# Channel product of a fused attention, gating and rotation block: from eight row tiles to seven block products per pair

## The chip, the cores and the metric

The kernel runs on one core of a Trainium2 chip, as one program in one launch. The metric is the device time of that core in microseconds. The kernel before took 833.74 us, the median of three runs (832.26 to 833.87).

## What is computed

The batch has B = 8 items of S = 576 tokens; the model width is 512 and everything is float32. Three stages follow each other. The reference, cut to what matters:

```python
p_packed = sm_attn(p, k, v)                 # attention of 32 packed queries per head
x = sm_attn(q, p_packed, p_packed)          # attention back to 576 tokens, 8 heads of 64

h = np.maximum(x @ w_in, 0.0)               # gating stage, d_ff = 1024
u, v = h[..., :512], h[..., 512:]
v_n = (v - mean(v)) / np.sqrt(var(v) + 1e-06)            # layer norm over the width
v_s = einsum('ts,bsd->btd', w_spatial, v_n) + b_spatial[None, :, None]
x = (u * v_s) @ w_out

theta = x @ w_theta                         # rotation stage
zr, zi = x * np.cos(theta), x * np.sin(theta)
u = x + einsum('ts,bsd->btd', w_tok_r, zr) + einsum('ts,bsd->btd', w_tok_i, zi)
return u + np.maximum(u @ w_ch, 0.0)        # the channel product is u @ w_ch
```

## The kernel before

Float32 precision is kept on TensorE by splitting: every operand is stored as a high part `h` (rounded to the matmul's format) and a low part `l = x - h`, and a product is three matmuls, h·h, h·l and l·h. Each split costs one ScalarE instruction for the high part (`hi`, L519) and one subtraction on VectorE or GpSimd for the low part (`lo`; all VectorE and GpSimd instructions bear the recorder's line, L507).

**First phase.** A loop over the eight batch items computes both attentions (`first`, `second`), the gating input product (`m_part`, `u_part`, `v_part`), the layer norm (inside `v_part`, whose inner function `rsq` finds 1/sqrt(var + eps) on five columns) and the spatial product (`g_part`), which goes out to a DRAM tensor `Gd`. In between, the weights of the later stages are converted from the float64 in which they arrive (`cvt_tasks`), split, combined and, as far as they are needed in blocks, stored to DRAM (`wr_part` to `Wd`; `wc_part` keeps `w_ch` split in SBUF as `WC`). The first 34 us are filled up with 70 matmuls on the identity that feed nothing (L1242).

**Second phase.** It works on four pairs of batch items (p = 0 to 3). A pair has nine row tiles of 128 rows: four of the first item (j = 0 to 3), one that holds the last 64 rows of both (j = 4), four of the second (j = 5 to 8). `X` makes x and theta of two tiles (`x_pair`: a 2x2 block product with seven instead of eight block products; the first six tiles go through `x_tile`), and `rotate` takes theta to cosine and sine: VectorE rounds the angle to whole turns by adding and subtracting a large constant (a TENSOR_SCALAR) and subtracts (a TENSOR_TENSOR), ScalarE takes Abs, Sin and Sin, two products follow. `mix(p, n)` with n = 1, 2, 6, 7, 4, 5, 3 is the token mixing of a pair in seven block products (`product`, weights loaded from `Wd` as `wg` tiles, operands split into `op` tiles). Its results are gathered in the `xs` tiles, which then hold u.

**The channel product.** `C(p, j)` takes one finished row tile of u. `turn` (L1598) transposes it by four TensorE instructions into a PSUM bank and splits it from there into a `uT` tile (high part on ScalarE, low part on VectorE). `chan` (L1608) multiplies: four blocks of the width times three terms are 12 matmuls, 128x128 by 512 columns, with `uT` as the stationary operand and `WC` as the moving one. VectorE then does max(., 0) + u in one instruction from PSUM and the tile is stored. There are 36 tiles, so 432 such matmuls.

**The order of the work.** Nothing is scheduled at run time. Every task is added to a plan (`P.add`, L432) and gets its place from a table of numbers, `PLACES` (L33), and, where two engines can do it, its engine from the table `ENGINES` (L351). `run` (L453) emits the tasks in order of their places, so the tables fix each engine's queue. `run` also ties a GpSimd task behind the VectorE task that stands ahead of it (the code gives as reason "order of the shared port"). Tiles come from pools (8 PSUM banks; `op` 5, `wg` 3, `xs` 13, `fa` 20, `tt` 2, `uT` 2); a task that needs a new tile waits until one is free.

```python
            for k in range(4):
                for x, y in ((0, 0), (1, 0), (0, 1)):
                    mm(ps.t, uT.t[:, x * 512 + k * 128:x * 512 + (k + 1) * 128], WC[y][:, k, :], m == 0, m == 11)
```

Of the kernel before, what the change touches and what calls it, by code (L numbers as in the profile page):

```python
# [21 lines left out]
NPAIR = B // 2  # L22
# [4 lines left out]
RSQRT_SEED = float(0x5F3759DF)  # L27
# [11 lines left out]
    "chan DVE": [  # L39
        1785, 1615, 1883, 1800, 1816, 1929, 1881, 2045, 1941, 2085, 2061, 2176, 2183, 2279, 2261, 2304, 2332, 2375,  # L40
        2419, 2483, 2526, 2593, 2671, 2748, 2631, 2752, 2780, 2869, 2831, 2833, 2876, 2875, 2880, 2891, 2867, 2887,
        2888],
    "chan mms": [
        1573, 1604, 1841, 1776, 1810, 1917, 1873, 1947, 1931, 2064, 2032, 2163, 2171, 2267, 2251, 2292, 2319, 2355,
        2410, 2434, 2510, 2577, 2660, 2708, 2625, 2745, 2721, 2754, 2779, 2828, 2850, 2866, 2873, 2886, 2855, 2878],
    "chan st": [
        1807, 1690, 1889, 1823, 1820, 1973, 2015, 2069, 1946, 2091, 2063, 2190, 2187, 2283, 2265, 2307, 2346, 2408,
        2421, 2521, 2531, 2596, 2712, 2749, 2633, 2782, 2784, 2883, 2834, 2838, 2879, 2885, 2884, 2892, 2881, 2890,
        2889],
    "cvt_tasks a": [  # L50
        65, 74, 42, 50, 164, 160, 174, 178, 241, 273, 349, 333, 339, 485, 407, 616, 470, 796, 814, 573, 882, 925,
        651, 1051, 1021, 673, 1144, 1292, 746],
# [58 lines left out]
    "load_tile DVE": [
# [10 lines left out]
    "m_part ACT": [  # L122
        120, 115, 157, 148, 216, 214, 234, 231, 323, 309, 305, 328, 478, 465, 463, 475, 640, 627, 629, 623, 783, 788,
# [389 lines left out]
def moe_kernel(ctx: ExitStack, tc, qT, kT, v, pT, w_in, wsT, bs, w_out,  # L513
# [1244 lines left out]
    for p in range(NPAIR):  # L1758
# [80 lines left out]
```

## Time and profile before

| | |
|---|---|
| median of three runs | 833.74 us (832.26 to 833.87) |
| profiled execution | 833.59 us, span from first to last instruction 831.6 us |
| granted TensorE clock | 0.999 of full speed (2.4 GHz) over the span |
| TensorE busy | 823.5 us, 99% of the span |
| VectorE busy | 631.3 us, 76% |
| ScalarE busy | 463.1 us, 56% |
| GpSimd busy | 218.9 us, 26% |
| DMA | 119 MB, 143 GB/s on average |

The span is cut by the profile into instructions of each engine; PE is TensorE, PEld its weight loads, DVE VectorE, ACT ScalarE, POOL GpSimd, SP the engine that issues the DMAs. A matmul's duration is longer than the distance to the next one, as they are pipelined, so what a matmul costs is read from a long row of them and not from its own duration. Identity matmuls and the like in full float32 count as two instructions in the profile.

### The profile page before, as it was taken

How to read it: one execution, taken by the hardware profiler on the slowest of the kernel's cores; microseconds unless marked ns; L12 is line 12 of the kernel's file. 1: busy time of each engine (PE TensorE's matmuls, PEld its weight loads, DVE VectorE, ACT ScalarE, POOL GpSimd, SP SyncE). 2: the span in 40 equal slices, each digit the busy share in tenths (PEclk: the TensorE clock that was granted, in tenths of full speed). 3: DMA queues.
4: the chain of work that ended last, by engine and by line, in shares of the span. 5: the costliest groups of instructions: out<-in, count | busy, mean ns of one | idle time of the engine just before them, and what ended most of it. 6: DMA issues, size and time to landing. Idle time of an engine off the chain costs nothing.

```text
span 831.6 us, 14720 instructions
## 1 busy us (share of the span) xinstructions
PE 823.5 (99%) x5490; PEld 684.9 (82%) x5490; DVE 631.3 (76%) x1260; ACT 463.1 (56%) x981; POOL 218.9 (26%) x176
## 2 busy tenths in 40 slices
PE   9999999999999999999999999999999999999998
PEld 7778888878787999887888888888888888888886
DVE  4998889988898895687886788854787756877534
ACT  4897767875585863774546355455553436434310
POOL 0342414224311311003122231233324134133310
PEclk9999999999999999999999999999999999999999
DMA  9986366577655158542061233333224233123412
GB/s 316 340 290 210 113 213 205 175 242 233 183 161 154 44 168 259 181 139 81 9 215 52 89 114 87 104 114 101 86 68 136 92 102 128 39 88 100 151 55 88
DMA packets 86859, 119.03 MB, mean 143 GB/s; under 512 B 10882, under 2 KB 57730, under 8 KB 86788
## 3 DMA queue, kind: packets, MB, share of 16 engines
q1 hardware_dynamic: 86788, 118.09, 44.9%
q8 instruction: 43, 0.70, 0.3%
q14 instruction: 28, 0.23, 0.1%
HBM read 88.38 MB, written 29.69 MB: 142 GB/s over the span
## 4 chain that ended last, share of the span: by engine, by line
PE 94%; DMA 2%; DVE 1%; ACT 1%; issue 1%; SPq 0%; POOL 0%; POOLq 0%; DVEq 0%
PE bank L525 91%; PE bank L1603 2%; DMA vr<-vL 1%; DMA WX<-Td 1%; PE bank L719 1%; DVE WX L507 1%; PE bank L746 0%; DMA Wd<-raw 0%; PE bank L1049 0%; POOL op L507 0%; DVE M L507 0%; DVE at L507 0%; PE bank L720 0%; DVE gs L507 0%; SPq L1199 0%
## 5 line engine op out<-in xcount | busy, mean ns | idle before, releaser
L525 PE MATMUL bank<-op,wg 128*128 128x512 f32 x672 | 174.7, 392 | 0.5 <-POOL op L507 0.5
L525 PE MATMUL bank<-WX,gp 128*128 128x512 f32 x630 | 155.4, 391 | 0.0
L525 PEld LDWEIGHTS bank<-op,wg 128*128 128x128 f32 x672 | 125.0, 188 | 26.2 <-POOL op L507 1.0
L525 PEld LDWEIGHTS bank<-WX,gp 128*128 128x128 f32 x630 | 117.6, 188 | 24.3
L507 DVE TENSOR_TENSOR xs<-bank,xs 128x256 f32<-128x256 f32 (+2 forms) x125 | 72.9, 591 | 71.6 <-PE bank L525 59.6
L525 PE MATMUL bank<-WS,VN 128*128 128x288 f32 x768 | 115.7, 298 | 0.0
L525 PEld LDWEIGHTS bank<-WS,VN 128*128 128x128 f32 x768 | 105.7, 188 | 8.6 <-issue 3.4
L525 PE MATMUL bank<-WC,uT 128*128 128x512 f32 x432 | 104.2, 391 | 0.0
L525 PEld LDWEIGHTS bank<-WC,uT 128*128 128x128 f32 x432 | 80.6, 188 | 16.6
L507 POOL TENSOR_TENSOR op<-fa,op 128x512 fp32r<-128x512 f32 x40 | 52.0, 1307 | 155.0 <-DVE op L507 70.6
L1451 ACT ACTIVATE xs<-bank 128x256 f32<-128x256 f32 x60 | 22.8, 380 | 107.6 <-PE bank L525 107.4
L519 ACT ACTIVATE op<-fa 128x512 fp32r<-128x512 f32 x96 | 58.6, 628 | 42.8 <-PE bank L525 26.5
L507 POOL TENSOR_TENSOR fa<-xs,fa 128x512 f32<-128x512 f32 x29 | 38.2, 1323 | 89.8 <-DVE fa L507 24.5
L525 PE MATMUL bank<-at,M 128*128 128x288 f32 x384 | 56.6, 299 | 0.0
L525 PE MATMUL bank<-M,at 128*128 128x512 f32 x224 | 55.5, 395 | 0.0
L525 PEld LDWEIGHTS bank<-at,M 128*128 128x128 f32 x384 | 52.1, 188 | 1.9 <-ACT ur L934 0.5
L507 DVE TENSOR_TENSOR op<-fa,op 128x512 fp32r<-128x512 f32 x56 | 42.4, 769 | 9.8 <-ACT op L519 9.4
L525 PEld LDWEIGHTS bank<-M,at 128*128 128x128 f32 x224 | 40.7, 188 | 8.8 <-issue 0.9
L519 ACT ACTIVATE uT<-bank 128x512 fp32r<-128x512 f32 x36 | 21.3, 596 | 46.8 <-PE bank L1603 28.8
L507 DVE TENSOR_TENSOR fa<-fa,fa 128x512 f32<-128x512 f32 x56 | 40.4, 722 | 4.2 <-POOL fa L507 2.7
L525 PE MATMUL bank<-op,WR 128*128 128x512 f32 x128 | 39.5, 390 | 0.0
L519 ACT ACTIVATE gp<-g 128x768 fp32r<-128x768 f32 (+1 forms) x30 | 28.2, 951 | 19.5 <-PE bank L525 18.9
(178 smaller groups left out, 1452.3 us busy)
## 6 DMA issues: line engine op xcount, KB each, us to landing
wg<-Wd SPq DMA_DIRECT2D x56, 512.0 KB, 4.1
kt<-kT SPq DMA_DIRECT2D x16, 576.0 KB, 7.0
q<-qT SPq DMA_DIRECT2D x16, 576.0 KB, 7.5
vr<-vL SPq DMA_DIRECT2D x16, 512.0 KB, 6.6
out<-xs SPq DMA_DIRECT2D x32, 256.0 KB, 2.7
g<-Gd SPq DMA_DIRECT2D x60, 128.0 KB, 3.1
Wd<-raw SPq DMA_DIRECT2D x56, 128.0 KB, 2.0
Gd<-gs SPq DMA_DIRECT2D x16, 288.0 KB, 2.3
```

The source lines that it names most:

```text
L507: self.made.append(f(*a, **k))
L519: A.activation(out=out, in_=in_, func=AF.Copy)
L525: PE.matmul(out, lhsT, rhs, start=start, stop=stop, skip_group_check=more)
L719: PE.transpose(p1.t[:, k * 128:(k + 1) * 128], a1.t[:, k * 128:(k + 1) * 128], ident)
L1451: A.activation(out=to[a].t[:, c], in_=bank.t[:, a * 256:(a + 1) * 256], func=AF.Copy)
L1603: PE.transpose(pt.t[:, d * 128:(d + 1) * 128], xs.t[:, d * 128:(d + 1) * 128], ident)
```

## The change

**Channel product of three pairs.** For p = 0, 1, 2 the eight row tiles j = 0 to 3 and 5 to 8 no longer go through `C`. A new function, `chan_pair`, transposes u of both items (32 TensorE transposes, as `turn` did), copies the result from PSUM to `xs` tiles, and treats it as a 2x2 block matrix (halves of the width by the two items). With w_ch as the other 2x2 block matrix, seven block products of 12 matmuls replace eight tiles of 12 matmuls. Four of the seven need sums of blocks of u (`sub7`), and four need sums of blocks of w_ch. The latter are made once in the first phase by `wc_pair` (which replaces `wc_part`), stored to a DRAM tensor `Cd`, and loaded as `wg` tiles. Sums of products are formed partly by accumulation in PSUM, partly by a ScalarE copy (`save`) and a VectorE addition (`gather`). The output of these rows is stored transposed and put right on the host by a copy; j = 4 and the whole last pair go the old way.

**The angle's rounding.** In `rotate`, ScalarE adds the large constant (`near`, Identity with a bias tile), and VectorE does the rest in one SCALAR_TENSOR_TENSOR; the sign is turned in the sine's scale.

**The layer norm's root.** ScalarE takes Ln and Exp (`root`), VectorE does one correction step instead of a seed and three steps; the table set with both functions is asked for at the start.

**The list anew.** `PLACES` and `ENGINES` are new for the whole kernel. The pools `fa` and `tt` are merged into `xs` (35 tiles).

```diff
+    def chan_pair(p, key):
+        u = {}
+        for o in range(2):
+            four = [xs[p, 5 * o + i] for i in range(4)]
+            for k in range(4):
...
+                def trs4(four=four, k=k, pt=pt):
+                    for i in range(4):
+                        PE.transpose(pt.t[:, i * 128:(i + 1) * 128], four[i].t[:, k * 128:(k + 1) * 128], ident)
+                P.add("PE", 0.37, trs4, key + k, r=four, new=[pt])
+                P.add("ACT", 0.62, lambda t=t, pt=pt: A.activation(out=t.t, in_=pt.t, func=AF.Copy), key + k + 1, r=[pt], new=[t])
+                u[o, k] = t
+        b11, b21, b12, b22 = ([u[o, 2 * n + kk] for kk in range(2)] for o in range(2) for n in range(2))
...
+        def prod7(k0, n0, load, x, ps, start, key):
...
+                P.add("SP", 0.6, lambda: SP.dma_start(out=wg.t.bitcast(F32), in_=Cd[load]), key - 6, r=[R_cd], new=[wg], size=0.524e6)
...
+            ops = [split(x[kk], P.res("op"), key - 4 + 0.7 * kk) for kk in range(2)]
+            for m in range(2):
+                for kk in range(2):
+                    def f7(m=m, kk=kk):
+                        o = ops[kk][0]
+                        three(ps[m].t, lambda y: lhs(kk, m, y), lambda y: o.t[:, y], start and not kk, kk == 1, not start)
...
+        def save(ps, key):
+            t = []
+            for m in range(2):
+                c = P.res("xs")
+                P.add("ACT", 0.62, lambda c=c, m=m: A.activation(out=c.t, in_=ps[m].t, func=AF.Copy), key, r=[ps[m]], new=[c])
...
+        def gather(c, ps, key):
+            for m in range(2):
+                P.add("DVE", 0.69, lambda m=m: V.tensor_tensor(out=c[m].t, in0=ps[m].t, in1=c[m].t, op=ALU.add), key,
+                      r=[ps[m], c[m]], w=[c[m]])
...
+        Aq, Yq, Cq = two(), two(), two()
+        prod7(0, 0, None, b11, Aq, True, key)
+        prod7(2, 0, None, b21, Yq, True, key + 2.7)
+        c = save(Yq, key + 6)
+        gather(c, Aq, key + 6.5)
+        done7(c, 0, 0, key + 7)
+        t = sub7(b12, b11, key - 2)
+        prod7(0, 0, 0, t, Cq, True, key + 5.4)
+        sub7(b22, t, key + 1, t)
+        prod7(0, 0, 1, t, Aq, False, key + 8.1)
+        t3 = sub7(b22, b12, key + 5)
+        e = save(Aq, key + 11)
+        prod7(0, 0, 2, t3, Aq, False, key + 10.8)
+        sub7(b21, t, key + 4, t)
+        c = save(Cq, key + 8)
+        gather(c, Aq, key + 14)
+        done7(c, 1, 1, key + 15)
+        prod7(2, 256, None, t, Aq, False, key + 13.5)
+        done7(None, 0, 1, key + 17, Aq)
+        prod7(0, 0, 3, b22, Cq, False, key + 16.2)
+        gather(e, Cq, key + 19)
+        done7(e, 1, 0, key + 20)
...
         mix(p, 3)
-        todo += [(p, 5), (p, 6), (p, 4)]
+        if p + 1 < NPAIR:
+            P.group = 10 * p + 9
+            chan_pair(p, clock + 2)
+            clock += 22
+            todo += [(p, 4)]
+        else:
+            todo += [(p, 5), (p, 6), (p, 4)]
...
+        def near():
+            A.activation(out=ab.t, in_=f.t, func=AF.Identity, bias=magic)
+        P.add("ACT", 0.62, near, key - 0.1, r=[f], new=[ab])
 
         def frac():
-            V.tensor_scalar(out=ab.t, in0=f.t, scalar1=MAGIC, scalar2=MAGIC, op0=ALU.add, op1=ALU.subtract)
-            V.tensor_tensor(out=f.t, in0=f.t, in1=ab.t, op=ALU.subtract)
-        P.add("DVE", 1.15, frac, key, r=[f], w=[f], new=[ab], port=True)
+            V.scalar_tensor_tensor(out=f.t, in0=ab.t, scalar=MAGIC, in1=f.t, op0=ALU.subtract, op1=ALU.subtract)
+        P.add("DVE", 0.7, frac, key, r=[ab, f], w=[f], port=True)
...
+        def root():
+            A.activation(out=t(), in_=cols(0, 10).rearrange("p (j c) -> p j c", c=2)[:, :, 1], func=AF.Ln, bias=lneps)
+            A.activation(out=y(), in_=t(), func=AF.Exp, scale=-0.5)
+        P.add("ACT", 0.5, root, key + 8.4, r=[st], w=[st])
```

**Where the order shows it.** TensorE, pair 0. Before, a tile of the channel product is four transposes and, ten instructions on, a row of 12 matmuls with `uT` as stationary operand (`xs` is the tile of u, `WC` the weight, `gp` and `WX` belong to `x_pair`, `z` and `WRR` to the mixing):

```order
L1603 MATMUL bank_171<-ident,xs_4089 128x128 x4
...
L525 MATMUL bank_166<-z_4235,WRR 128x512 x3
L525 MATMUL bank_173<-WC_72,uT_4239 128x512 x2
L525 MATMUL bank_173<-WC_73,uT_4239 128x512
L525 MATMUL bank_173<-WC_72,uT_4239 128x512 x2
L525 MATMUL bank_173<-WC_73,uT_4239 128x512
...
```

Of the change, the same place: groups of three matmuls on an `op` tile (split transposed u), with `WC` or a `wg` tile loaded from `Cd`, mixed with matmuls of `x_pair` and one old-style transposition of tile j = 4:

```order
L555 MATMUL bank_175<-op_4079,WC_75 128x512
L555 MATMUL bank_175<-op_4079,WC_76 128x512
L555 MATMUL bank_175<-op_4079,WC_75 128x512
L1675 MATMUL bank_173<-ident,xs_4095 128x128 x4
L555 MATMUL bank_172<-WX_3637,gp_3639 128x512
...
L555 MATMUL bank_176<-op_3902,wg_4258 128x512 x3
L555 MATMUL bank_176<-op_4078,wg_4258 128x512 x3
L555 MATMUL bank_169<-op_3902,wg_4258 128x512 x3
L555 MATMUL bank_169<-op_4078,wg_4258 128x512 x3
L555 MATMUL bank_171<-op_3903,wg_4260 128x512 x3
```

The transposes are as many as before (32 for the eight tiles of a pair); the matmuls with 512 columns behind them are 84 where 96 stood.

VectorE, the same stretch of the change: what stands between the transposed blocks and those matmuls. `xs<-xs,xs` are the sums of blocks, `op<-xs,op` low parts of a split, `xs<-bank` reads of PSUM, `z` belongs to the mixing of the next pair:

```order
L537 TENSOR_TENSOR xs_4264<-xs_4094,xs_4091 128x512
L537 TENSOR_TENSOR z_4257<-xs_4084,z_4257 64x512
L537 TENSOR_TENSOR xs_4083<-xs_4089,xs_4087 128x512
L537 TENSOR_TENSOR op_3902<-xs_4264,op_3902 128x512
L537 TENSOR_TENSOR xs_4264<-xs_4271,xs_4264 128x512
L537 TENSOR_TENSOR op_4078<-xs_4083,op_4078 128x512
L537 TENSOR_TENSOR xs_4268<-xs_4097,xs_4268 128x512
L537 TENSOR_TENSOR xs_4081<-xs_4271,xs_4094 128x512
L537 TENSOR_TENSOR op_3903<-xs_4264,op_3903 128x512
L537 TENSOR_TENSOR xs_4086<-bank_175,xs_4086 128x512
L537 TENSOR_TENSOR xs_4090<-bank_171,xs_4090 128x512
```

Before, VectorE had one low part and one max-and-add per tile here, both from PSUM; now sums and low parts from SBUF stand close together.

SP, the first loads of the program. Before, the value tiles `vr` of the first item stand ahead of most of the weight `w_in`:

```order
L688 DMA kt_113<-kT 128x2x576
L693 DMA vr_114<-vL 128x4x256
L694 DMA vr_114<-vL 64x256
L999 DMA wth<-w_in 128x1024 x2
L999 DMA woT<-w_in 128x1024
```

Of the change:

```order
L721 DMA kt_116<-kT 128x2x576
L1034 DMA woT<-w_in 128x1024
L1034 DMA wth<-w_in 128x1024 x2
L726 DMA vr_117<-vL 128x4x256
L727 DMA vr_117<-vL 64x256
```

Three loads of `w_in` moved ahead of the first `vr`.

## Rows read from the trace of the kernel before

**Rows 1.** The page: span, and busy time, share and instructions of each engine

```profile
span 831.6 us, 14720 instructions
...
PE 823.5 (99%) x5490; PEld 684.9 (82%) x5490; DVE 631.3 (76%) x1260; ACT 463.1 (56%) x981; POOL 218.9 (26%) x176
```

**Rows 2.** The page: chain that ended last, share of the span by engine

```profile
PE 94%; DMA 2%; DVE 1%; ACT 1%; issue 1%; SPq 0%; POOL 0%; POOLq 0%; DVEq 0%
```

**Rows 3.** Windows: length, PE, PEld, DVE, ACT, POOL busy (count), clock, DMA

```profile
0.00:40.00 40.00, 38.13 (x430) 29.56 (x431) 28.41 (x66) 24.33 (x61) 7.97 (x13) 1.00 0.99 332
...
80.00:340.00 260.00, 258.73 (x2375) 220.70 (x2374) 223.15 (x535) 176.44 (x393) 68.42 (x54) 1.00 0.56 178
...
600.00:700.00 100.00, 100.00 (x454) 82.82 (x453) 71.24 (x123) 49.28 (x97) 28.50 (x23) 1.00 0.32 96
```

**Rows 4.** Waits of PE: the view without four small waits, together 1.5 us

```profile
PE bank L525 <- POOL ident masks.py:199: 1.4, 1, 1.4
PE bank L525 <- ACT vf L876: 0.8, 1, 0.8
PE bank L525 <- POOL op L507: 0.5, 1, 0.5
```

**Rows 5.** Timeline of PE in the second phase: start, length, instruction, count

```profile
399.11 2.88 PE L525 MATMUL bank<-WC,uT 128*128 128x512 f32 x12
...
404.55 4.24 PE L525 MATMUL bank<-op,wg 128*128 128x512 f32 x18
```

**Rows 6.** Groups by line: count, busy us, mean ns; the channel product

```profile
L525 PE MATMUL bank<-WC,uT 128*128 128x512 f32 x432 | 104.2, 391 | 0.0
```

**Rows 7.** Groups by line: the instructions of 512 columns beside TensorE

```profile
L519 ACT ACTIVATE op<-fa 128x512 fp32r<-128x512 f32 x96 | 58.6, 628 | 42.8 <-PE bank L525 26.5 <-POOL fa L507 8.0 <-DVE fa L507 7.7
L507 POOL TENSOR_TENSOR op<-fa,op 128x512 fp32r<-128x512 f32 x40 | 52.0, 1307 | 155.0 <-DVE op L507 70.6 <-ACT op L519 25.8 <-DVE fa L507 24.6
L507 DVE TENSOR_TENSOR op<-fa,op 128x512 fp32r<-128x512 f32 x56 | 42.4, 769 | 9.8 <-ACT op L519 9.4
L507 DVE TENSOR_TENSOR fa<-fa,fa 128x512 f32<-128x512 f32 x56 | 40.4, 722 | 4.2 <-POOL fa L507 2.7
...
L507 DVE TENSOR_TENSOR uT<-bank,uT 128x512 fp32r<-128x512 f32 x36 | 24.6, 686 | 18.4 <-ACT uT L519 18.3
L507 DVE SCALAR_TENSOR_TENSOR xs<-bank,xs 128x512 f32<-128x512 f32 (+1 forms) x37 | 24.6, 671 | 13.7 <-PE bank L525 13.6
...
L1496 ACT ACTIVATE fa<-fa 128x512 f32<-128x512 f32 x36 | 22.5, 626 | 23.0 <-DVE fa L507 22.9
...
L507 DVE TENSOR_SCALAR fa<-fa 128x512 f32<-128x512 f32 x36 | 16.3, 453 | 8.8 <-ACT fa L1451 4.7 <-issue 1.9 <-ACT fa L1367 1.8
```

**Rows 8.** Groups by line: small instructions and table loads

```profile
L507 DVE SCALAR_TENSOR_TENSOR ln<-ln 128x5 f32<-128x5 f32 x56 | 9.2, 165 | 1.9
...
L1497 ACT ACT_TABLE_LOAD x1 | 1.3, 1283 | 0.0
...
L1238 ACT ACTIVATE one<-halfpi 128x1 f32<-128x1 f32 x1 | 0.2, 203 | 0.0
```

**Rows 9.** Windows: the second phase, and its 28 us with most VectorE work

```profile
736.00:764.00 28.00, 28.00 (x135) 23.25 (x134) 24.78 (x39) 14.27 (x27) 9.34 (x7) 1.00 0.32 101
...
360.00:832.00 472.00, 467.27 (x2130) 386.50 (x2128) 329.55 (x547) 213.22 (x411) 126.64 (x97) 1.00 0.32 99
```

**Rows 10.** Timeline: the end of the program

```profile
819.37 8.45 PE L525 MATMUL bank<-WC,uT 128*128 128x512 f32 x36
...
827.86 0.69 DVE L507 SCALAR_TENSOR_TENSOR xs<-bank,xs 128x512 f32<-128x512 f32 x1 [1.96 <-PE bank L525]
```

**Rows 11.** Timeline of PE: the first use of `vr`, the first product of `v_part`

```profile
12.31 0.90 PE L525 MATMUL bank<-vr,aT 128*32 128x64 f32 x40 [0.51 <-ACT aT L725]
...
33.94 3.92 PE L525 MATMUL bank<-M,at 128*128 128x512 f32 x16
```

**Rows 12.** DMA issues: count, KB each, median us to landing

```profile
wg<-Wd SPq DMA_DIRECT2D x56, 512.0 KB, 4.1
```

More of the change, by code (lines that the diff above doesn't have):

```diff
@@ L203 @@
+    "rotate near": [
+        1431, 1472, 1459, 1448, 1530, 1526, 1573, 1581, 1638, 1631, 1756, 1701, 1765, 1759, 1986, 1941, 2061, 2039,
+        2196, 2117, 2201, 2193, 2363, 2383, 2458, 2444, 2507, 2584, 2659, 2616, 2667, 2644, 2888, 2831, 2938, 2944],
+    "save ACT": [
+        1881, 1874, 1919, 1915, 1904, 1925, 2314, 2309, 2345, 2337, 2331, 2353, 2783, 2785, 2819, 2815, 2828, 2821],
     "second load_q": [
-        25, 30, 209, 154, 355, 354, 506, 441, 536, 533, 691, 768, 912, 887, 1097, 1007],
+        27, 30, 179, 180, 283, 264, 376, 379, 613, 609, 719, 715, 947, 943, 1058, 1012],
@@ L293 @@
+        1167, 1287, 1310, 1297],
+    "wc_pair ACT": [
+        891, 955, 948, 1344, 1377, 1384],
+    "wc_pair SP": [
+        850, 895, 1299, 1331],
+    "wc_pair any": [
+        910, 971, 954, 1370, 1382, 1389],
+    "wc_pair store_c": [
+        961, 1392],
+    "wc_pair sums": [
+        929, 1378],
     "win_part ld": [
-        16, 22, 9, 12, 81, 76, 86, 70],
+        22, 3, 10, 7, 93, 101, 86, 102],
     "wo_part ACT": [
-        359, 325, 613, 445],
+        508, 308, 577, 405],
     "wo_part ld": [
-        206, 243, 233, 289],
+        247, 153, 273, 237],
@@ L366 @@
+    "split any": ("VVGGGVVGVGVVVGVVGGVVVVGGGGVVVGVVVVVVGVVVGVVVGVGVVGVVVVVVVGGGVGVVGVGGVGVVGGVVGVVVGVVGGVVGVGGVGVVV"
+        "VVVGVVGGGGGVGVVGVVGGGVGVVVVVVGGVVVVVVVVVVVVVVVVVVVVVVVGGGV"),
+    "v_part any": "VVGGVGGVVVVGGGGVVVGGVVGGVVGGGVVVVVVVVVVV",
+    "v_part norm": "VAVAAVAVVAVAAAAVAAVVAVAAVAVVVVVAVAAVVAAA",
+    "wc_pair any": "VGVVVV",
+    "wc_pair sums": "VV",
+    "wr_part any": "GGGV",
+    "wr_part sums": "GVGV",
+    "wr_parts any": "GGGGVGGGG",
     "ws_part any": "GGGGGG",
-    "wx_split any": "GVGVGGVV",
+    "wx_split any": "GVVVVGGV",
@@ new lines, in wc_pair, with sums, store_c @@
+    def wc_pair(kk, key):
+        gs = []
+        for n in range(2):
+            k = kk + 2 * n
+            raw, g, rh = P.res("raw"), P.res("cvg"), Res()
+            P.add("SP", 0.6, lambda raw=raw, k=k: SP.dma_start(out=raw.t[:, 0:1024].bitcast(I32).rearrange("p (n w) -> p n w", w=2),
+                                                               in_=w_ch[k * 128:(k + 1) * 128]), key - 5, new=[raw], size=524e3, after=wr_last)
+            gv = lambda g=g: g.t[:, 0:DM]
+            cvt_tasks(raw, DM, gv, key, [raw], new=[g])
+            P.add("ACT", 0.62, lambda k=k, gv=gv: hi(WC[0][:, k], gv()), key + 2, r=[g], w=[rh, R_WC])
+            P.add(TT, 0, lambda e, k=k, gv=gv: lo(WC[1][:, k], gv(), WC[0][:, k], ENG[e]), key + 3, r=[g, rh], w=[R_WC], port=True)
+            gs.append((raw, g))
+            key += 4
+        (raw, g), (rawi, gi) = gs
+        sm = P.res("raw")
+        q = lambda n: sm.t[:, 256 * n:256 * n + 256]
+        def sums(e):
+            e = ENG[e]
+            e.tensor_tensor(out=q(2), in0=g.t[:, 0:256], in1=g.t[:, 256:512], op=ALU.subtract)
+            e.tensor_tensor(out=q(0), in0=g.t[:, 256:512], in1=gi.t[:, 256:512], op=ALU.add)
+            e.tensor_tensor(out=q(1), in0=q(0), in1=g.t[:, 0:256], op=ALU.subtract)
+            e.tensor_tensor(out=q(3), in0=gi.t[:, 0:256], in1=q(1), op=ALU.subtract)
+        P.add({"DVE": 1.75, "POOL": 3.0}, 0, sums, key + 2, r=[g, gi], new=[sm], port=True)
+        wr_last[:] = P.tasks[-1:]
+        hh, ll = (lambda: raw.t[:, 0:1024].bitcast(F32R)), (lambda: sm.t[:, 0:1024].bitcast(F32R))
+        P.add("ACT", 1.1, lambda: hi(hh(), sm.t[:, 0:1024]), key + 4, r=[sm], w=[raw])
+        P.add({"POOL": 2.5, "DVE": 1.25}, 0, lambda e: lo(ll(), sm.t[:, 0:1024], hh(), ENG[e]), key + 5, r=[raw], w=[sm], port=True)
+        def store_c():
+            for x, t in enumerate((raw.t, sm.t)):
+                for n in range(4):
+                    SP.dma_start(out=Cd[n, :, 2 * kk:2 * kk + 2, x, :],
+                                 in_=t[:, 256 * n:256 * n + 256].rearrange("p (m t) -> p m t", m=2))
+        P.add("SP", 4.8, store_c, key + 6, r=[raw, sm], w=[R_cd], size=1.05e6)
@@ L1431, in x_pair @@
         gp, rg = loaded.pop(-n)
-        f = [P.res("fa") for _ in range(2)]
+        f = [P.res("xs") for _ in range(2)]
         A1, B1, C1 = (P.res("bank") for _ in range(3))
@@ L1498, in rotate @@
               r=[ab], w=[ab])
-        P.add("ACT", 0.62, lambda: A.activation(out=f.t, in_=f.t, func=AF.Sin, scale=2 * math.pi), key + 0.2, r=[f], w=[f])
+        P.add("ACT", 0.62, lambda: A.activation(out=f.t, in_=f.t, func=AF.Sin, scale=-2 * math.pi), key + 0.2, r=[f], w=[f])
         for q, zf in enumerate((ab, f)):
@@ L1766, in moe_kernel @@
             more(nx + 1)
+        more((9 * p + 6) // 2)
         mix(p, 2)
@@ L1837 @@
     r = run_bass_kernel_spmd(nc, [arrays], core_ids=[0])
-    return np.ascontiguousarray(r.results[0]["out"])
+    o = np.array(r.results[0]["out"])
+    for b in range(B - 2):
+        o[b, 0:512] = o[b, 0:512].T.copy()
+    return o
```

301 lines of the change are left out of this document (160 added, 141 removed), and 227 rows, old and new, of the table PLACES.

## Prediction

> **What bounds the kernel now.** I first read the busy shares on the page: TensorE is busy for 823.5 of 831.6 us, the next engine, VectorE, for 631.3 [rows 1]. A share is an average, so the windows come second. They show what sort of bound it is: in 600 to 700 us TensorE is busy for all 100.00 us, VectorE for 71.24, ScalarE for 49.28, GpSimd for 28.50, and even in the first 40 us only 1.87 us of TensorE are idle [rows 3]. The chain that ended last agrees: 94% of it is TensorE [rows 2]. Third, the waits of TensorE: seven in the whole program, 1.4 us at the very start and six of 0.2 to 0.8 us; one of them, 0.5 us, is in the second phase [rows 4]. But a matmul's modelled end can hide a late start, so I checked the distance between neighbours in the timeline: 18 matmuls of 512 columns take 4.24 us of which the last one's own 0.391 us [rows 6] is a tail, so (4.24 - 0.39) / 17 = 0.2265 us each; the 12 of a channel tile give (2.88 - 0.39) / 11 = 0.2264 [rows 5]. Every long row I looked at in the second phase has this pitch, at a granted clock of 1.00 [rows 3], the 2.4 GHz level. So the reader should see a TensorE that is never kept waiting: a matmul taken away is worth its 0.2265 us, and everything else is worth nothing as long as it stays hidden.
>
> **TensorE.** Before, 432 matmuls of the channel product. After: 12 tiles remain on the old way (j = 4 of three pairs, nine of the last), 12 x 12 = 144, and three pairs have 7 products x 12 = 84 each, 252. Together 396, so 36 fewer. The transposes are equally many, 4 per tile before, 32 per pair after. The order shows no other difference in TensorE's instructions. 36 x 0.2265 = **8.15 us** less, all of it on the path.
>
> **VectorE and GpSimd, second phase.** These counts come from the order of both kernels. VectorE loses 36 TENSOR_SCALAR of 0.453, 24 low parts of `uT` of 0.686 and 18 max-and-adds from PSUM of 0.671: 16.3 + 16.5 + 12.1 = 44.9 us. It gains 32 low parts of `op` (0.769), 38 differences of blocks and the like (0.722), 18 max-and-adds from SBUF (not in the trace; 0.722 taken from the two-input subtraction, the nearest) and 18 additions from PSUM (0.686): 24.6 + 27.4 + 13.0 + 12.3 = 77.3 [rows 7]. Net +32.4 us. VectorE had 329.55 busy of the last 472 us [rows 9]; it becomes 362 of some 464, 78%. GpSimd gets 10 low parts more and 14 products and differences fewer at 1.307 or so, about -5 us. I cost all this at nothing: TensorE hides it as long as VectorE is in time where the new work is dense (rival 1).
>
> **ScalarE.** 42 more high parts (0.628), 36 `near` (not in the trace; 0.626 of the Abs of the same size), 42 copies out of PSUM against 24 `uT` high parts (18 x 0.626): 26.4 + 22.5 + 11.3 = 60 us [rows 7]. From 213 to 273 of 464 us, 59% [rows 9]. Nothing on the path. In `rotate` the chain gets longer by the 0.626 of `near` less the 0.453 of the TENSOR_SCALAR, 0.17 us and one change of engine; its consumers stand several microseconds of matmuls later.
>
> **Layer norm's root.** VectorE has 56 fewer of the 5-column instructions: 56 x 0.165 = 9.2 us over eight items, and ScalarE 16 small ones of about 0.2 us more [rows 8]. Per item the chain falls from 12 x 0.165 = 2.0 to 5 x 0.165 + 2 x 0.2 = 1.2 us, plus a hop. TensorE does not wait there: in 80 to 340 us it is idle for 1.27 us in all [rows 3]. So the gain lies between 0 and all six waits after the start, 2.8 us together [rows 4]; a loss of the same size is as possible, since new places can make a wait as well as remove one. I take 0. The two functions could each want their own table: at 1.283 us a load [rows 8], 16 loads would put 20.5 us on ScalarE inside that chain. The order of the changed program has two loads, as before, one at the start and one at the first Sin, so I leave that out. The Trainium skill (ScalarE: Activation LUTs, section "Table sets: the hidden batching unit") says that one set holds both exp and ln; no run here shows it yet.
>
> **The first loads.** Three loads of `w_in` move ahead of `vr` on SP. At 332 GB/s [rows 3] their 1.57 MB are 4.7 us. The first use of `vr` at 12.31 us waited for ScalarE, not for the load [rows 11]; the tables put 34 of the 70 filling matmuls ahead of it where 19 stood, so it is planned later. What counts is the first product of `v_part` at 33.94 us [rows 11], and the weights it needs come earlier. Between -1.4 us (all but the unavoidable of the 1.87 idle) and +4.7; I take 0, because both orders put the same 70 fillers ahead of that product.
>
> **`w_ch` in blocks.** `wc_pair` adds two groups of sums, a high and a low part of 1024 columns each and 16 small stores in the first phase, some 6 us on VectorE against the 9.2 just saved. In the second phase 12 more loads of `wg`, 4.1 us each to landing [rows 12], at a DMA share of 0.32 [rows 9]; they stand on SP ahead of their product by 8 us of matmuls or more. The end of the program keeps its form: last matmul, one VectorE instruction, a store, so the 3.7 us from 827.86 to the span's end stay [rows 10].
>
> **Sum.** The profiled execution took 833.59 us, 831.6 of them the span; it lies 0.15 below the median. 833.6 - 8.15 = 825.4, against the median 833.74 - 8.15 = 825.6. I predict 825.5.
>
> **Rivals.**
>
> *1. VectorE is late in the dense stretch.* From the last mixing product of pair 0 to the sixth of its seven block products I counted in the order 24 groups of three matmuls, five products of `x_pair`, five transpositions and a tile: 28.0 us of TensorE. VectorE has 26.1 us of work there by the durations of rows 7, 93%. For it: that is more than the busiest 28 us before, 24.78 us. Against it: those 24.78 us went by with TensorE at 28.00 [rows 9]. And each product's operand is formed well ahead: the first difference of blocks needs 0.722 + 0.628 + 0.769 = 2.1 us after the copy, and over 11 us of matmuls stand in between. If one such chain is laid bare per pair, 3 x 2.1 = 6.4 us come back: 831.8 us; half of it, 828.6.
>
> *2. VectorE and GpSimd cannot overlap, and together become the bound (slower).* GpSimd's low parts waited 70.6 us for VectorE [rows 7], since the order holds them. In the stretch above GpSimd has five tasks, 6.6 us; if none of it overlaps with VectorE, the two need 32.7 us for 28.0 of TensorE: 4.7 us x 3 pairs = 14 us, 839.5 us. It decides against the change from 3.3 us per pair on (8.15 + 1.7 in three parts). Against it: 7.9 of VectorE's 26.1 us read PSUM; if only the rest excludes GpSimd, 18.2 + 6.6 = 24.8 of 28.0 fit. The Trainium skill (GPSIMD Engine Reference, section "1. Specifications") says that GpSimd's SBUF interfaces are shared with VectorE and contended by VectorE instructions with two SBUF inputs, which speaks against this change, as it turns PSUM reads into SBUF ones; by that rule the smaller sum, 24.8, holds.
>
> *3. The new list also removes waits.* If the six later waits of 2.8 us go too, 822.7 us. For it: the shorter root, 3 us less on VectorE in the first phase. Against: nothing ties the waits to it.
>
> *4. The list loses at the start what the matmuls save.* If `vr` is late by the full 4.7 us and one chain is bare, 825.5 + 4.7 + 2.1 = 832.3: no difference. The cover of the fillers speaks against it.
>
> **How the numbers follow.** My forecast, 36 matmuls and stalls within 2 us either way: 0.70. Rival 1: 0.12, rival 2: 0.06, rival 3: 0.08, rival 4: 0.04. The range takes in rivals 1 to its half and beyond and 3: 822.5 to 830.0, leaving out 0.2 at most. A difference of 0.2%, 1.7 us, is about what a measurement of this kernel can tell. Faster: forecast, rival 3 and nearly all of rival 1, 0.89. Within it: rival 4 and the end of rival 1, 0.05. Slower: rival 2, 0.06.
>
> **What would show it.** Right: 396 channel matmuls, busy time of TensorE near 815.4 us, the pitch of 0.2265 us in the stretches of the seven products, no wait over 1 us behind the transposes, VectorE near 78% from 360 us on, two table loads. Wrong: waits of TensorE for `op` (low part) or for `xs` (sums), several per pair, would be rival 1 or 2; a first `v_part` product later than 34 us with waits on `vr` would be rival 4; more than two table loads would overturn the root.

## The result, and the profile after

The changed kernel took 826.08 us, the median of four runs (825.60 to 826.82), against 833.81 us of the kernel before on the same chip (832.26 to 833.90): a ratio of 0.9915 (95% interval 0.990 to 0.993), 7.7 us less. Forecast were 825.5 us and a range of 822.5 to 830.0. The profiled execution took 825.63 us, 823.9 of them the span.

The page of the changed kernel: span, busy times and chain (the kernel before: [rows 1], [rows 2]).

```profile
span 823.9 us, 14828 instructions
...
PE 814.1 (99%) x5454; PEld 677.4 (82%) x5454; DVE 661.0 (80%) x1250; ACT 523.8 (64%) x1088; POOL 217.9 (26%) x173
...
PE 92%; DVE 3%; DMA 2%; ACT 1%; issue 1%; POOL 0%; SPq 0%; DVEq 0%; POOLq 0%
```

TensorE has 5454 instructions, 36 fewer, and 9.4 us less busy time. VectorE and ScalarE have gained 30 and 61 us and hide them. Where that holds is read from the windows (length, busy time and count of PE, PEld, DVE, ACT, POOL, clock, DMA share, GB/s, as in [rows 3]):

```profile
0.00:40.00 40.00, 36.85 (x400) 29.23 (x404) 28.12 (x66) 23.61 (x56) 9.35 (x14) 1.00 0.96 312
80.00:340.00 260.00, 259.52 (x2356) 221.91 (x2356) 214.84 (x486) 179.72 (x409) 71.52 (x56) 1.00 0.62 189
360.00:400.00 40.00, 37.57 (x164) 30.13 (x163) 38.10 (x57) 32.01 (x62) 9.20 (x7) 1.00 0.35 114
400.00:500.00 100.00, 100.00 (x461) 83.03 (x460) 81.35 (x130) 63.35 (x120) 31.58 (x24) 1.00 0.36 106
600.00:700.00 100.00, 100.00 (x451) 82.86 (x450) 79.82 (x138) 62.55 (x121) 27.88 (x22) 1.00 0.44 130
360.00:824.00 464.00, 457.70 (x2086) 378.26 (x2084) 369.58 (x590) 270.96 (x510) 119.48 (x90) 1.00 0.37 115
```

From 400 us on TensorE is full until the last tile. The one weak stretch of the second phase is its first 40 us, 37.57 us busy, with VectorE at 38.10. The waits of TensorE (total, times, longest, us) say for what:

```profile
PE bank L555 <- ACT xs L1520: 2.2, 2, 1.5
...
PE bank L555 <- DVE M L537: 1.0, 1, 1.0
PE bank L555 <- DMA vr<-vL: 0.5, 1, 0.5
...
PE bank L555 <- DVE xs L537: 0.2, 1, 0.2
```

Three of them, 2.4 us, stand together where the mixing begins; they are new. The timeline of TensorE there (start, length, instruction, count, wait before it), and farther on a long row of block products and the last row of the program:

```profile
360.60 2.88 PE L555 MATMUL bank<-op,wg 128*128 128x512 f32 x12
...
372.19 4.39 PE L555 MATMUL bank<-WX,gp 128*128 128x512 f32 x18 [1.46 <-ACT xs L1520]
377.33 1.65 PE L555 MATMUL bank<-WX,gp 128*128 128x512 f32 x6 [0.75 <-ACT xs L1520]
379.21 1.65 PE L555 MATMUL bank<-WX,gp 128*128 128x512 f32 x6 [0.23 <-DVE xs L537]
...
470.07 5.60 PE L555 MATMUL bank<-op,wg 128*128 128x512 f32 x24
...
811.71 8.42 PE L555 MATMUL bank<-WC,uT 128*128 128x512 f32 x36
```

The first row begins the mixing. Before, it began here:

```profile
362.35 1.52 PE L525 MATMUL bank<-op,wg 128*128 128x512 f32 x6
```

In both programs 3372 TensorE instructions stand ahead of this place. So the changed program reaches the mixing 1.75 us earlier, with none of the 36 matmuls saved yet. The 24 block-product matmuls give (5.60 - 0.39) / 23 = 0.2265 us each, the old pitch. The last 36 matmuls, the same in both programs, begin 819.37 - 811.71 = 7.66 us earlier. The account is -8.15 for the matmuls, -1.75 for the earlier mixing and +1.9 for the waits (2.4 against 0.5 before), -8.0 in all against the 7.66 us measured; 0.3 us are not traced to a place.

### The profile page after: what moved, and what is told of

It is laid out like the page before. It is cut to its first block, busy times and chain, and to the rows that moved or that the text cites. A ratio compares the mean times of both kernels' runs of the same rounds, so it can differ in the third digit from the quotient of the medians.

```text
span 823.9 us, 14828 instructions
## 1 busy us (share of the span) xinstructions
PE 814.1 (99%) x5454; PEld 677.4 (82%) x5454; DVE 661.0 (80%) x1250; ACT 523.8 (64%) x1088; POOL 217.9 (26%) x173
## 4 chain that ended last, share of the span: by engine, by line
PE 92%; DVE 3%; DMA 2%; ACT 1%; issue 1%; POOL 0%; SPq 0%; DVEq 0%; POOLq 0%
PE bank L555 89%; PE bank L1717 1%; DVE xs L537 1%; DMA vr<-vL 1%; DMA WX<-Td 1%; PE bank L752 1%; DVE sm L537 1%; PE bank L1675 1%; DVE raw L537 0%; DVE t L537 0%; PE bank L779 0%; SPq L1265 0%; ACT xs L1562 0%; PE bank L1084 0%; ACT xs L1568 0%
## 5 line engine op out<-in xcount | busy, mean ns | idle before, releaser
L555 PE MATMUL bank<-op,wg 128*128 128x512 f32 x816 | 207.1, 390 | 0.0
L555 PEld LDWEIGHTS bank<-op,wg 128*128 128x128 f32 x816 | 152.5, 188 | 31.3
L549 ACT ACTIVATE op<-xs 128x512 fp32r<-128x512 f32 x154 | 92.7, 628 | 55.4 <-PE bank L555 35.0
L537 POOL TENSOR_TENSOR op<-xs,op 128x512 fp32r<-128x512 f32 x53 | 70.6, 1338 | 163.3 <-DVE op L537 49.5
L537 POOL TENSOR_TENSOR xs<-xs,xs 128x512 f32<-128x512 f32 x40 | 53.6, 1342 | 176.7 <-DVE xs L537 50.2
L537 DVE TENSOR_TENSOR xs<-xs,xs 128x512 f32<-128x512 f32 x120 | 87.3, 755 | 5.3 <-ACT xs L1719 1.8
L537 DVE TENSOR_TENSOR op<-xs,op 128x512 fp32r<-128x512 f32 x101 | 71.1, 721 | 22.8 <-ACT op L549 22.0
L537 DVE SCALAR_TENSOR_TENSOR xs<-xs,xs 128x512 f32<-128x512 f32 x54 | 40.6, 764 | 15.5 <-ACT xs L1562 15.2
L555 PE MATMUL bank<-WC,uT 128*128 128x512 f32 x144 | 34.5, 392 | 0.0
L537 DVE TENSOR_TENSOR gp<-g,gp 128x768 fp32r<-128x768 f32 (+1 forms) x30 | 33.8, 1148 | 0.3 <-ACT gp L549 0.3
```

What stands on the lines that cost most here:

```text
L537: self.made.append(f(*a, **k))
L549: A.activation(out=out, in_=in_, func=AF.Copy)
L555: PE.matmul(out, lhsT, rhs, start=start, stop=stop, skip_group_check=more)
```

## The experiments

Every time below is a median, and every ratio is to the kernel before on the same chip. Line numbers shift a little between the variants. The runs were made on three chips. The kernel before took 833.38 us on the first (the changed kernel again, copy moved, rounding undone, root undone), 833.83 on the second (matmuls put back, small parts on the old kernel, GpSimd's share moved, low parts twice) and 832.93 on the third (the three with the loads moved). Runs on different chips are better compared by their ratios. First the changed kernel once more, as the measure of scatter.

> The changed kernel once more, to compare the other runs of this call with. Both theories: 826 us, within 0.6.

Measured: 826.02 us (825.74 to 826.20), 0.9908 (0.9893 to 0.9922). Differences of less than about 0.7 us are not read in what follows. The profile of this run has the three waits at the start of the mixing again, the first of them 1.89 us instead of 1.46; so one profile does not fix such a wait to better than 0.4 us.

**The 36 matmuls put back.** In each pair three of the seven products get the fourth term l·l, 4 matmuls in each and so 12 a pair, on operands that are there anyway.

```diff
...
-   three(ps[m].t, lambda y: lhs(kk, m, y), lambda y: o.t[:, y], start and not kk, kk == 1, not start)
+   three(ps[m].t, lambda y: lhs(kk, m, y), lambda y: o.t[:, y], start and not kk, kk == 1 and not fourth, not start)
+   if fourth:
+       mm(ps[m].t, lhs(kk, m, 1), o.t[:, 1], False, kk == 1, not start)
```

> 36 matmuls put back into the changed kernel: in the first three of the seven products of each pair a fourth term (low part times low part) stands behind the three, 12 matmuls of 512 columns a pair. Nothing else moves. Theory A (every matmul is worth its pitch): 826.1 + 36 x 0.2265 = 834.2 us, as before the change. Rival B (the gain comes from the list and the lighter VectorE): the extra matmuls fill waits, 828 us or less.

Measured: 834.48 us (833.20 to 837.19), 1.0007 (0.9996 to 1.0018): the time of before. The page:

```profile
PE 823.0 (99%) x5490; PEld 684.7 (82%) x5490; DVE 660.4 (79%) x1250; ACT 524.2 (63%) x1088; POOL 218.2 (26%) x173
```

TensorE has the 5490 instructions of before, and VectorE and ScalarE have the work of the changed kernel. So the matmuls are worth 834.48 - 826.02 = 8.5 us, or 8.2 by the two ratios (1.0007 and 0.9908), within the scatter of the 8.15 forecast, and all else in the change nets to nothing. The profiled execution, 835.61 us, is longer than the median: its first wait at the start of the mixing is 2.43 us, and the 18 matmuls behind it took 5.99 us instead of 4.39, as the granted clock fell (last section).

**The small parts on the old kernel.** The kernel before, with its old list, gets rounding and root on ScalarE, each half a place ahead of its partner on VectorE.

```diff
+PLACES["rotate near"] = [x - 0.5 for x in PLACES["rotate frac"]]
+PLACES["v_part root"] = [x - 0.5 for x in PLACES["v_part rsq"]]
...
```

> The kernel before with the rounding and the layer norm's root on ScalarE alone, on the old list. Theory A: TensorE was never kept waiting by these, no difference, 833 to 834.5 us. Rival B: 2 to 3 us faster, 831 us.

Measured: 834.22 us (833.18 to 835.72), 1.0007 (0.9998 to 1.0017). The mixing begins at 362.25 us, against 362.35 in the kernel before. VectorE fell from 631.3 to 606.9 us, which bought nothing:

```profile
PE 824.4 (99%) x5490; PEld 684.5 (82%) x5490; DVE 606.9 (73%) x1170; ACT 488.9 (59%) x1033; POOL 218.8 (26%) x176
```

**The rounding undone on the changed kernel.** VectorE again takes the TENSOR_SCALAR and the TENSOR_TENSOR; the list is otherwise the new one.

```diff
-        P.add("ACT", 0.62, near, key - 0.1, r=[f], new=[ab])
...
-            V.scalar_tensor_tensor(out=f.t, in0=ab.t, scalar=MAGIC, in1=f.t, op0=ALU.subtract, op1=ALU.subtract)
+            V.tensor_scalar(out=ab.t, in0=f.t, scalar1=MAGIC, scalar2=MAGIC, op0=ALU.add, op1=ALU.subtract)
+            V.tensor_tensor(out=f.t, in0=f.t, in1=ab.t, op=ALU.subtract)
...
```

> The angle's rounding back on VectorE in the changed kernel, all else kept. Theory A: VectorE gets 36 x 0.45 = 16 us more, ScalarE 36 x 0.72 = 26 us less, TensorE waits at most where the mixing begins, where VectorE is full: 825 to 827.5 us. Rival B (the moved small parts made the room that the gain needed): waits in each of the dense stretches, 829 us or more.

Measured: 825.91 us (825.24 to 826.89), 0.9908 (0.9895 to 0.9921). No difference, though VectorE then has 680.6 us. The time does not depend on where the rounding stands.

**The root undone on the changed kernel.** VectorE takes the seed and three steps again.

```diff
-        P.add("ACT", 0.5, root, key + 8.4, r=[st], w=[st])
...
+            for _ in range(3):
+                V.tensor_tensor(out=t(), in0=y(), in1=y(), op=ALU.mult)
...
```

> The layer norm's root back on VectorE in the changed kernel, all else kept. Theory A: hidden in the first phase, 826 to 827 us. Rival B (the shorter root gave the 1.75 us by which the mixing now begins earlier): 0.8 us longer in each of eight items, if half of them are bare 3 us, 829 us.

Measured: 828.38 us (827.52 to 831.89), 0.9947 (0.9931 to 0.9963): 2.4 us slower than the changed kernel, between theory A and rival B. This part is not free on the new list. The profiled execution was a long one, 831.89 us, and shows two things. TensorE's timeline:

```profile
362.56 2.88 PE L555 MATMUL bank<-op,wg 128*128 128x512 f32 x12
...
376.08 7.28 PE L555 MATMUL bank<-WX,gp 128*128 128x512 f32 x18 [3.39 <-ACT xs L1518]
```

and its windows of 4 us:

```profile
374.00:378.00 4.00, 1.92 (x5) 1.54 (x6) 3.09 (x7) 3.67 (x8) 0.25 (x1) 0.68 0.00 0
378.00:382.00 4.00, 4.00 (x11) 3.13 (x10) 3.20 (x6) 1.78 (x4) 1.25 (x2) 0.50 0.00 0
382.00:386.00 4.00, 3.25 (x13) 2.32 (x13) 3.24 (x7) 2.56 (x6) 1.06 (x1) 0.96 0.00 0
```

The mixing begins at 362.56 instead of 360.60 us, and the wait that was 1.46 is 3.39 us. Behind it the granted clock fell to 0.50, the 1.2 GHz level, and 18 matmuls took 7.28 us instead of 4.39. The timed executions spread accordingly: four lie at 827.5 to 828.4 with a mean granted clock of 0.999 to 1.000, two at 831.2 and 831.9 with 0.998 and 0.995. The median, 2.4 us above the changed kernel, is thus one of those without the fall of the clock. Two causes were left for the 2.4 us: eight later layer norms, or the wait at the transition behind them. The next three runs go after the transition.

**The copy out of PSUM moved forward.** The product that waits 1.46 us accumulates into a bank that ScalarE has still to copy out. Here the product ahead of it and that copy get earlier places.

```diff
+for _n, _a, _b in (("prod mms", 1528, 1525.5), ("out copy", 1535, 1526.5)):
+    PLACES[_n] = [_b if x == _a else x for x in PLACES[_n]]
```

> Two numbers of the list changed: the ScalarE copy out of the first product of the fourth x_pair stands ahead of the two roundings and the Abs of the tiles before. Theory A (TensorE is bound by the count of its matmuls, and what is missing of the 8.15 us is waits where the mixing begins): the wait of 1.46 us at 370 us goes, 1.0 to 1.5 us less, about 824.8. Rival (the wait comes from the late sums of weights, not from the queue of ScalarE; or the two tiles that are now late take it over): the wait stays or shows up within 10 us behind, 826 us.

Measured: 826.26 us (825.23 to 827.34), 0.9911 (0.9898 to 0.9924). My theory fell. The wait became small and the next ones grew, to 2.9 us in all:

```profile
371.39 3.02 PE L558 MATMUL bank<-WX,gp 128*128 128x512 f32 x12 [0.43 <-ACT xs L1523]
375.38 1.65 PE L558 MATMUL bank<-WX,gp 128*128 128x512 f32 x6 [0.97 <-ACT xs L1523]
377.78 1.65 PE L558 MATMUL bank<-WX,gp 128*128 128x512 f32 x6 [0.75 <-ACT xs L1523]
380.19 1.65 PE L558 MATMUL bank<-WX,gp 128*128 128x512 f32 x6 [0.76 <-DVE xs L540]
```

All that is there stands in ScalarE's queue, and ahead of it ScalarE waited for the loads of the weight sums `WX`, in this run 0.41, 0.85 and 0.42 us.

**Those loads moved forward.** In the changed kernel ScalarE waits three times for them, 1.07 us in all:

```profile
363.22 1.06 ACT L549 ACTIVATE WX<-WX 128x1024 fp32r<-128x1024 f32 x1 [0.27 <-DMA WX<-Td]
...
365.20 1.06 ACT L549 ACTIVATE WX<-WX 128x1024 fp32r<-128x1024 f32 x1 [0.38 <-DMA WX<-Td]
366.69 1.06 ACT L549 ACTIVATE WX<-WX 128x1024 fp32r<-128x1024 f32 x1 [0.42 <-DMA WX<-Td]
```

On SP they stand behind the last load of `g` for a later group of tiles, which leaves only at 356.96 us:

```profile
356.96 0.36 SPq L1453 DMA_DIRECT2D g<-Gd  x1
357.43 2.61 SPq L1265 DMA_DIRECT2D WX<-Td  x4
```

```diff
+for _n, _a, _b in (("load_pair ld", 1482, 1501.5), ("load_pair sums", 1504, 1523.5)):
...
+    PLACES[_n] = [_b if x == _a else x for x in PLACES[_n]]
```

> The changed kernel, with two places of the list moved: the four loads of the weight sums (WX from Td) go ahead of the loads of g for the fifth group of tiles on SP's queue, and the block sums of that g go behind the last low part of the weight sums on VectorE. In the changed kernel the last of those g loads left SP only at 356.96 us, the WX loads right behind it at 357.43, and ScalarE then waited 0.27 + 0.38 + 0.42 us for WX. Theory A (the 2.4 us of waits at the start of the mixing come from the late weight sums): the WX loads leave SP up to 0.9 us earlier, ScalarE's 1.1 us of waits for WX shrink, the wait of 1.46 us before the product becomes 0.3 to 0.8, the waits at 370 to 380 us fall to 1 to 1.7 us in all, and the time is 824.6 to 825.6. Rival B (ScalarE's queue of copies, roundings and splits sets the pace there whatever the loads do, as in the run with the copy first): the waits stay at 2 us or more in all, and the time stays at 826.0 +- 0.4. Rival C: the g loads, now later, make the products that use that g late, a new wait for gp behind 380 us of 1 us or more; 826.5 to 828.

Measured: 825.44 us (824.70 to 826.15), 0.9903 (0.9888 to 0.9918). The loads leave at 356.46, and the waits at 370 to 380 us fall from 2.4 to 1.9:

```profile
371.56 4.37 PE L559 MATMUL bank<-WX,gp 128*128 128x512 f32 x18 [0.89 <-ACT xs L1524]
376.68 1.66 PE L559 MATMUL bank<-WX,gp 128*128 128x512 f32 x6 [0.75 <-ACT xs L1524]
378.57 1.66 PE L559 MATMUL bank<-WX,gp 128*128 128x512 f32 x6 [0.23 <-DVE xs L541]
```

ScalarE's waits for `WX` fell from 1.07 to 0.33 us, the long wait of TensorE by 0.6 of its 1.46, and the other two waits are untouched, so theory A holds in part. That is one profile against one; the other pair on record, the changed kernel again and the last run below, gives the same step at another level, 1.89 against 1.31 with ScalarE's waits at 1.50 and 0.50. The time is 0.6 us below the changed kernel, too little to be told from it.

**The root undone, with those loads moved forward.** Both edits together.

> The layer norm's root back on VectorE (which alone gave 828.4, with a wait of 3.4 us at the start of the mixing, a granted clock of 0.50 at 378 to 382 us behind it, and the mixing 2.0 us later than in the changed kernel), together with the move of the WX loads ahead of the g loads. Theory A (most of what the root costs there lies at the transition: the wait and the clock that fell after it): the wait of 3.4 us falls below 2.5, the clock stays at 1.00, and the time is 826.5 to 827.5. Rival B (the root's cost lies in the first phase, the mixing simply begins 2 us later): the time stays 1.8 us or more above the run with the loads first alone, near 827.5 to 828.5, whatever the wait does.

Measured: 828.21 us (827.92 to 828.90), 0.9936 (0.9923 to 0.9950), 2.8 us above the run with the loads alone. The long wait is down to 1.47 us, and its six executions lie within 1 us. The 2.8 us are still there, because the mixing begins at 363.16 instead of 360.54 us:

```profile
363.16 2.88 PE L559 MATMUL bank<-op,wg 128*128 128x512 f32 x12
```

So rival B holds: what the root costs on this list lies in the first phase. The windows of 80 to 340 us, first with the loads moved alone, then with the root undone too, and one of TensorE's waits in the second:

```profile
80.00:340.00 260.00, 259.53 (x2356) 221.95 (x2355) 214.48 (x486) 179.71 (x409) 71.50 (x56) 1.00 0.61 189
```

```profile
80.00:340.00 260.00, 258.08 (x2346) 220.28 (x2345) 226.44 (x534) 173.33 (x390) 71.47 (x56) 1.00 0.61 189
...
PE bank L559 <- DVE gs L541: 1.3, 1, 1.3
```

With the root undone TensorE gets 10 instructions less done in this stretch, which at the pitch of the matmuls that run at its end (0.2265 us) is 2.3 of the 2.6 us. Its busy time shows only 1.4 us of it, 1.3 of them the wait for VectorE's `gs`; the rest is hidden in rows that count as busy.

**GpSimd's share put on VectorE.** The 20 GpSimd tasks of the seven products go to VectorE.

```diff
+        if name in ("split any", "TTop any") and self.group in (9, 19, 29):
+            t.eng = "DVE"
```

> The 20 differences and low parts that GpSimd has inside the seven products of the three pairs go to VectorE, at the same places. Theory A with a margin on VectorE (it is busy for some 26 of 28 us in a stretch, but neighbours overlap): 6 or 7 of 0.72 us more in a stretch, that is 4.5 us against 2 to 4 of room, 826 to 829 us. Rival C (VectorE is at its edge): 4 us come back per pair, 834 us or more. Rival 2 of the prediction (VectorE and GpSimd shut each other out): faster than the changed kernel, as each move takes 1.31 from GpSimd and gives 0.72.

Measured: 825.34 us (824.44 to 826.07), 0.9894 (0.9880 to 0.9909), below the range expected for a margin and, if the 0.7 us to the changed kernel are more than scatter, on rival 2's side; by the ratios the two cannot be told apart. TensorE is busy for all of 400 to 800 us. VectorE has margin in the dense stretches, but this run hardly tests it: the 20 instructions are 14.4 us at 0.72, and VectorE's busy time rose only from 661.0 to 666.9 us. Its other work took 8.5 us less while GpSimd had 27.2 us less to do:

```profile
PE 814.0 (99%) x5454; PEld 677.2 (82%) x5454; DVE 666.9 (81%) x1270; ACT 523.8 (64%) x1088; POOL 190.7 (23%) x153
```

**The low parts computed twice.** The 42 low parts of the seven products are issued twice.

```diff
...
+   P.add(TT, 0, lambda e: [lo(o.t[:, 1], x.t, o.t[:, 0], ENG[e]) for _ in range(many)], key + 0.1, r=[x, h], w=[l], port=True)
```

> The low part of every split operand of the seven products is computed twice (42 more, on the engine that has it). Theory A with a margin: 14 more per pair, about 10 us of VectorE and 5 of GpSimd in some 30 us, more than the room there is: 832 to 845 us. If it is 826 to 828, VectorE has far more room than its busy share says and rival C was never near. Rival C: 14 x 0.9 = 12 us a pair, 860 us.

Measured: 848.92 us (847.16 to 851.15), 1.0179 (1.0157 to 1.0201), a little past the upper end expected. The waits of TensorE show the mechanism of rival 1, provoked:

```profile
PE bank L555 <- DVE op L537: 6.0, 6, 1.3
PE bank L555 <- POOL op L537: 4.8, 3, 2.3
...
PE bank L555 <- DVE xs L537: 1.8, 3, 0.8
```

So the margin is real but not wide: 30 us more on VectorE and 22 on GpSimd, in these stretches alone, cost 23 us. The waits in the view add up to 20.3 us against 6.0 in the changed kernel, 14 of the 23; the rest lies in a longer busy time of TensorE, 822.4 against 814.1 us, in part with a lower clock (0.83 granted in 600 to 620 us).

**Both gains together.** Loads first, and GpSimd's share on VectorE.

> The same move of the loads and sums, and the 20 GpSimd tasks of the seven block products put on VectorE, as in the run with all of them on VectorE (825.3 there). If both gains are real and add up: 824.2 to 825.0, below every kernel so far. If the 0.7 us of that run was scatter: the time of the run with the loads first, within 0.4. If VectorE, with both, runs out of time in the dense stretches: waits for op or xs behind 400 us and 826 or more.

Measured: 825.51 us (824.94 to 826.07), 0.9902 (0.9888 to 0.9917). They do not add up; the three variants at 825.3 to 825.5 are, for this measurement, the changed kernel.

## Why the prediction was right

**TensorE, 8.15 us.** Right, in count (396: 144 with `uT`, 108 with `WC` and 144 with loaded weights) and in pitch (0.2265), and it is the cause of the difference, since the run with the 36 back has the time of before.

**VectorE in the second phase.** 369.58 us instead of 362, 80% instead of 78%. The sum was short because durations of the trace before were used: the SCALAR_TENSOR_TENSOR taken as 0.722 measured 0.764, 2.3 us over its 54, and the block sums of `g`, which the change doesn't touch, 0.489 on average instead of 0.434, which alone is 3.3 us. The last 2 us are not traced. These are the groups (count, busy us, mean ns, idle before), the first of them from the kernel before:

```profile
L507 DVE TENSOR_TENSOR g<-g 128x256 f32<-128x256 f32 x60 | 26.0, 434 | 3.6 <-DMA g<-Gd 1.9
```

```profile
L537 DVE SCALAR_TENSOR_TENSOR xs<-xs,xs 128x512 f32<-128x512 f32 x54 | 40.6, 764 | 15.5 <-ACT xs L1562 15.2
...
L537 DVE TENSOR_TENSOR g<-g 128x256 f32<-128x256 f32 x60 | 29.3, 489 | 3.4 <-DMA g<-Gd 1.7
...
L1562 ACT ACTIVATE xs<-xs,magic 128x512 f32<-128x512 f32 x36 | 25.7, 719 | 3.2 <-DVE xs L537 2.9
```

Costed at nothing, it was nothing behind 400 us, where TensorE is full.

**ScalarE.** 270.96 us against 273, a total nearer than its terms: `near` took 0.719 us and not 0.626, 3.3 us more, and the copies out of PSUM 0.595 and not 0.626, 0.6 us less on the 18 counted; what else was less is not traced. The nearest row was not the Abs but the cosine of the same tile, which has a bias tile too: 0.719 in this trace. The Trainium skill (ScalarE: Activation LUTs, section "What ACT_TABLE_LOAD costs") says that each pointer operand, such as a bias column, adds about 93 ns to an ACTIVATE; the trace agrees, 719 - 626 = 93.

**The root, taken as 0.** The bracket "0 to 2.8" held the value, but the step that led to 0 was half right. On the old list it is 0. On the new list undoing it costs 2.4 to 2.8 us: the mixing begins at 360.2 to 360.9 us in all nine profiles of that list with the root on ScalarE, and at 362.56 and 363.16 in the two without. So the 1.75 us by which the mixing begins earlier are there only with the root on ScalarE, and only with the new list. That the new list was laid for the short chain would explain it; no run shows that apart. I had read the waits of TensorE in the first phase as the limit of the gain. But the view's waits leave out what is hidden in rows that count as busy (part of the 2.6 us above), and an edit's price on a fixed list is not its price on another. Two table loads remained, and Ln and Exp took 0.30 and 0.21 us on five columns:

```profile
L922 ACT ACTIVATE ln<-ln,lneps 128x5 f32<-128x5 f32 x8 | 2.4, 300 | 0.9 <-DVE ln L537 0.8
L923 ACT ACTIVATE ln<-ln 128x5 f32<-128x5 f32 x8 | 1.7, 208 | 0.3
...
L1306 ACT ACT_TABLE_LOAD x1 | 1.3, 1283 | 0.7 <-PEq L2001 0.7
L1571 ACT ACT_TABLE_LOAD x1 | 1.3, 1283 | 0.0
```

The Trainium skill (ScalarE: Activation LUTs, section "Table sets: the hidden batching unit") says that one set holds both exp and ln. The trace agrees: Ln and Exp alternate eight times, with two table loads in the whole program.

**The first loads.** Taken as 0. The first product of `v_part` came at 34.03 us against 33.94, and the wait for `vr` at 39.81 was 0.52 us. Rival 4 did not occur. The lower bound of -1.4 was too wide: of the 1.87 us idle, 1.36 are the wait at the very start, for `ident` from GpSimd, which no load ends; so 0.5 at most was to be had.

**Waits I did not forecast.** The prediction looked for new waits in the stretches of the seven products, where there are none. They came where the new list starts the mixing, 2.4 us, and the earlier start of the mixing gave as much back. That the total met the forecast to 0.6 us is luck in this part: two terms that the prediction took as 0, the root and the start of the mixing, were about 2 us each with opposite signs.

**The rivals.** 1: 28 us of VectorE hold 27.6 us of work, but they lie at 374 to 402 us, where the mixing has begun, and not among the seven products; there no chain was laid bare. 2: the contention exists (below), but leaves enough room. 3: waits went and waits came.

## What to carry to other kernels

Where one engine has no waits, count its instructions: 36 matmuls by their measured pitch were the net result, and where TensorE had no waits, some 90 us of work more on other engines weighed nothing. In a kernel with a planned order, an edit's price is that of the edit with its list: the same root was worth 0 on one list and over 2 us on another, so test each part by undoing it on the new list and by adding it to the old. When a wait is shortened, look at the next two before counting the gain; here one queue passed the delay on.

## What the runs showed of the hardware

**VectorE beside GpSimd.** The four block sums of `g` took 3.78 us while GpSimd's two low parts ran, and 1.79 us in the run that moved them to a place where GpSimd was idle. The timelines of VectorE and GpSimd in the changed kernel, then of VectorE with the sums moved:

```profile
360.01 3.78 DVE L537 TENSOR_TENSOR g<-g 128x256 f32<-128x256 f32 x4
...
363.70 1.29 DVE L537 TENSOR_TENSOR xs<-xs,xs 128x512 f32<-128x512 f32 x2
...
360.31 2.74 POOL L537 TENSOR_TENSOR op<-xs,op 128x512 fp32r<-128x512 f32 x2 [1.97 <-DVE op L537]
```

```profile
359.95 2.38 DVE L541 TENSOR_TENSOR xs<-xs,xs 128x512 f32<-128x512 f32 x2
...
367.90 1.79 DVE L541 TENSOR_TENSOR g<-g 128x256 f32<-128x256 f32 x4
```

In the second kernel two other subtractions stand beside GpSimd instead, and take 2.38 us where a pair alone took 1.29 (the second row). That pair ran while the DMA moved some 370 GB/s, against 330 during the slow sums, so the loads are not the cause. All have two inputs in SBUF. The rule weighed in rival 2 (the Trainium skill, GPSIMD Engine Reference, section "1. Specifications": the two share their SBUF interfaces, and VectorE instructions with two SBUF inputs contend) agrees in kind; the size, 2.0 us lost beside 2.74 us of GpSimd, is this trace's.

**The clock after a wait.** In the profile with a wait of 3.39 us (the root undone) the granted clock was 0.68, 0.50 and 0.96 in the stretches of 4 us from 374, 378 and 382 us (the wait ended at 376.08). The wait cost its own time and 2.9 us more on the next 18 matmuls. In the profile with the 36 matmuls back the wait was 2.43 us and ended at 372.84; the clock was 0.97 and 0.60 in the stretches from 370 and 374 us, and the 18 matmuls took 1.6 us more. In the profiles with waits of 1.46, 1.47, 1.89 and 1.93 us at the same place it stayed at 1.00.
